# Four batches through a gated block and a spectral block: first blocks of all batches, then second blocks, with split weights kept in DRAM

## The chip, the core and the metric

One core of a Trainium2 chip runs the whole kernel. The metric is the device time of one execution in microseconds (us); lower is better. Kernels are compared by the median of several executions.

## What is computed

Batch B = 4, sequence S = 768, model width 384 (8 heads of 48), in three steps, all in float32:

```python
# attention: a decayed state per head
f = 1 / (1 + exp(-f_logit))
for t in range(S):
    state = f[:, :, t, :, None] * state + einsum('bhd,bhde', k[:, :, t], v[:, :, t])
    y[:, :, t] = einsum('bhd,bhde->bhe', q[:, :, t], state)
# first block
h = gelu_tanh(x @ w_in)                         # 384 -> 1024
u, v = h[..., :512], h[..., 512:]
v_n = layernorm(v) * g_ln
v_s = einsum('ts,bsd->btd', w_sg, v_n) + b_sg   # mixes tokens, 768 x 768
x = x + (u * v_s) @ w_out                       # 512 -> 384
# second block
theta = x @ w_theta
y = einsum('ts,bsd->btd', w_tok_r, x * cos(theta)) + einsum('ts,bsd->btd', w_tok_i, x * sin(theta))
u = x + y
out = u + maximum(u @ w_ch, 0)
```

w_in, w_out, w_theta, w_tok_r, w_tok_i and w_ch reach the chip as 64-bit floats, w_sg as 32-bit ones.

## The kernel before, in words

**Split products.** A float32 product is made of three matmuls of fp32r parts: every operand is split into a rounded part (hi, an ACT cast) and what is left over (lo, a DVE subtraction), and `mm3` (lines 771 to 785) adds hi x hi, hi x lo and lo x hi in PSUM (lines 779, 780, 781). A split weight is twice as large as the weight itself.

**Weights.** `load_f32` (411) brings a weight tile in; 64-bit ones land in a raw buffer and are turned into float32 by an ACT operation (431) and four DVE ones (432 to 435). `load_split` (437) adds the cast (444) and the subtraction (445). `w_in` and `w_out` are split once and stay in SBUF (`win`, `wout`). The mixing weights don't fit: they pass as 36 tiles of 128 x 384 for each batch (`order`, 394: 12 tiles `g` of w_sg, 24 of w_tok_r and w_tok_i), through `stream` (481) into the five slots of `st`. The 24 are decoded once by `decode` (474), from a raw slot into a float32 slot `wt` (two slots), and written to `scratch1` in DRAM by POOL's queue; each batch then loads them (192 KB, `dt<-scratch`) and splits them anew, as it does with the tiles of w_sg (`dt<-in_w_sgT`). So 144 tiles are split in all. `channel_weights` (460) makes w_theta and w_ch for the first batch that needs them, keeps both parts in `scratch2`, and loads them from there for the others into the one slot `wmid`.

**A first block** (`block1`, 926) runs p1 (v half of x @ w_in with gelu and layernorm, six token tiles), p2(0), p3(0) (token mixing, 12 matmuls on each streamed tile), p2(1), p4(0) (w_out and the residual), p3(1), and hands back p4(1) as a call, which the next block runs in its middle (`before`). The layernorm's power is a POOL operation (975). **A second block** (`block2`, 1003) runs theta (sine and cosine, an ACT chain of lines 881 to 888 and DVE products of line 891), p6(0) and p6(1) (token mixing, 216 matmuls in all, 9 on each streamed tile), and p7 with the output DMA. x lives in `xst` (two slots for each half of the sequence), its split parts in `X`. **Attention** of a batch is two halves of four head pairs (`unit`, 585, one mask multiply of line 657 in each); its results go to `xst` by DMAs of POOL (752).

**Order.** Nothing is ordered by hand. The operations of all engines are created with a due time `vt` (the due times of a block's products add up in `mm3`), and `schedule` (173) plays them on a model of the engines: each engine takes, of the operations that can start at its next free moment, the one with the earliest due time, so work without hurry fills idle time. A DMA of POOL is counted as 1.05 us of issue, and lands 0.65 + bytes / 360e3 + 0.95 us later (lines 283 to 290, 400). The engines then run their lists strictly in this order, each instruction behind the one before it. The buffers of one kind are taken in the order in which they were created.

Lines 1042 to 1076 say what is created, in which order: attention of batch 0; first block of 0, with attention of 1 spread beside it; first block of 1; decoding, spread from the start of batch 0's block over 80% of both blocks; second block of 0; second block of 1, with attention of 2 beside it; then batch 2, both blocks, with attention of 3 beside them; then batch 3. The two calls that decide:

```python
        rest = one1(rest, False)
...
            decode(pl, g, i, v + (pl.vt - v) * at / 100)
        two(rest, True)
...
        two1(nothing, True)
        x = spread(2, v)
```

A second program branch (`general`, 1089) for very small decays is built too and is not run with these inputs.

Of the kernel before, what the change touches and what calls it, by code (L numbers as in the profile page):

```python
# [8 lines left out]
F32 = mybir.dt.float32  # L9
# [39 lines left out]
WARM_GAP = 0.3  # L49
N_DT = 3  # L50
N_W = 2
# [3 lines left out]
MID = 90.0  # L55
# [268 lines left out]
def body(tc, ctx, att, qkv, flog, w_in, g_ln, w_sgT, b_sg, w_out, w_theta, w_rT, w_iT, w_ch, out):  # L324
# [86 lines left out]
    def load_f32(pl, g, dst, src, vt, after=(), background=False):  # L411

        n = src.shape[-1]
        d, get = dst
        if src.dtype != I64:
            dma(pl, "SP", n * 512, lambda: nc.sync.dma_start(get(), src), after, w=[d], vt=vt - 3)
            return
# [19 lines left out]
    def load_split(pl, g, hi, lo, his, src, vt, scale=None, after=(), background=False):  # L437

        n = src.shape[-1]
        t = pl.buf(g.w32 if background else g.dt, [P, TH])  # L440
        load_f32(pl, g, (t, lambda: t.t[:, :n]), src, vt, after, background)
        if scale is not None:
            pl.op("ACT", a1(n), lambda: nc.scalar.mul(t.t[:, :n], t.t[:, :n], scale), [], [t], vt=vt)
        pl.op("ACT", a1(n), lambda: nc.scalar.copy(his()[0], t.t[:, :n]), [t], [], hi, vt=vt)  # L444
        pl.op("DVE", v1(n), lambda: nc.vector.tensor_sub(his()[1], t.t[:, :n], his()[0].bitcast(F32)), [t, *hi], [], lo, vt=vt)  # L445

    def weights_in(pl, g, cs, vt):
        for c in cs:
            for k in range(NK):
                cc, b = slice(c * WC, (c + 1) * WC), [g.win[k][c]]  # L450
                load_split(
                    pl, g, b, b, lambda k=k, cc=cc: (win[:, 0, k, cc], win[:, 1, k, cc]), w_in[k * P : (k + 1) * P, cc], vt,
                )

    def weights_out(pl, g, vt):
        for k in range(ND):
            b = [g.wout[k]]
            load_split(pl, g, b, b, lambda k=k: (wout[:, 0, k], wout[:, 1, k]), w_out[k * P : (k + 1) * P], vt)

    def channel_weights(pl, g, i, b, vt):  # L460
        w = pl.buf(g.wmid, [P, 2, NK, DM], F32R)
        if b == 0:
            src, scale = ((w_theta, 1.0 / (2.0 * math.pi)), (w_ch, None))[i]
            for k in range(NK):
                load_split(
                    pl, g, [w], [w], lambda k=k: (w.t[:, 0, k], w.t[:, 1, k]), src[k * P : (k + 1) * P], vt, scale,
                    background=True,
                )
            dma(pl, "POOL", P * 9216, lambda: nc.gpsimd.dma_start(scratch2[i], w.t.bitcast(F32)), [w], [g.scr2[i]], vt=vt)
        else:  # L470
            dma(pl, "SP", P * 9216, lambda: nc.sync.dma_start(w.t.bitcast(F32), scratch2[i]), [g.scr2[i]], [w], vt=vt)
# [294 lines left out]
    def moe(pl, g, xst, get, wmid, out_b, pace, first=False):  # L766
# [34 lines left out]
        def residual(ps, hf, k, resplit=True):  # L801
# [48 lines left out]
        def p4(hf, gb, resplit):  # L850
            for c in range(NK):
# [5 lines left out]
                residual(ps, hf, c, resplit)  # L857
# [68 lines left out]
        def block1(before, resplit):  # L926
# [72 lines left out]
            p4(0, g0, resplit)  # L999
            g1 = p3(1, u1, vtiles)  # L1000
            return lambda: p4(1, g1, resplit)
# [26 lines left out]
    with tc.manual_schedule():  # L1028
# [15 lines left out]

        def blocks(b, x):
            get = lambda pl, i: stream(pl, g, i, pl.vt - LEAD)
            wmid = lambda pl, i: mids.pop() if mids else channel_weights(pl, g, i, b, pl.vt - LEAD * 1.5)
            return moe(pl, g, x, get, wmid, out[b], PACE if b + 1 < B else 1.0, b == 0)
# [5 lines left out]
        v = pl.vt  # L1054
        one, two = blocks(0, x)
        rest = one(nothing, False)
        x = spread(1, v + (pl.vt - v) * LATE / 100)
        one1, two1 = blocks(1, x)
        rest = one1(rest, False)
        mids = []  # L1060
        for i in range(2 * NS, len(order)):
            at = BG_FROM + (BG_TO - BG_FROM) * (i - 2 * NS) / (len(order) - 2 * NS)
            if not mids and at >= MID:
# [156 lines left out]
```

## Time and profile before

| | |
|---|---|
| median of 3 runs | 686.87 us (684.5 to 708.57) |
| the profiled execution's own time | 685.9 us |
| its span, first to last instruction | 684.2 us |
| mean granted TensorE clock | 0.974 of full |
| TensorE matmul busy | 626.0 us (91%) |
| VectorE busy | 512.5 us (75%) |
| ScalarE busy | 398.1 us (58%) |
| GpSimd busy | 82.4 us (12%) |

| stretch of the span (us) | what TensorE runs in it |
|---|---|
| 0 to 77.1 | attention of batch 0, decoding of w_in, first p1 tiles of batch 0, and p2(0) |
| 77.1 to 174.8 | the rest of batch 0's first block but p4(1), attention of batch 1 |
| 174.8 to 243.2 | first block of batch 1, p4(1) of batch 0 |
| 243.2 to 314.1 | second block of batch 0, p4(1) of batch 1, some attention of batch 2 |
| 314.1 to 403.0 | second block of batch 1, the rest of batch 2's attention |
| 403.0 to 471.2 | first block of batch 2, half of batch 3's attention |
| 471.2 to 550.0 | second block of batch 2, p4(1), the other half |
| 550.0 to 607.0 | first block of batch 3 |
| 607.0 to 684.2 | second block of batch 3 with p4(1) and theta (to 630.3), p6 (to 668.0), p7, last stores |

The engines are PE (TensorE matmuls), PEld (its weight loads), DVE (VectorE), ACT (ScalarE), POOL (GpSimd) and SP (which only issues DMAs). PEclk is the TensorE clock that was granted, 1.00 being the full 2.4 GHz. An instruction's line is that of the helper that records it. Matmuls are pipelined: of 128x384 ones each shows some 0.34 us, and one ends every 0.17 us.

### The profile page before, as it was taken

The numbers are of one execution on the slowest core, as the hardware profiler recorded it, in microseconds if no ns is written. First come the engines' busy times: TensorE is split into PE (matmuls) and PEld (weight loads), VectorE is DVE, ScalarE is ACT, GpSimd is POOL, SyncE is SP. The second block draws the span as 40 slices with busy tenths as digits, with TensorE's granted clock in tenths as the row PEclk, the third lists the DMA queues.
The fourth block names the chain that finished last, engine by engine and source line by source line (L and its number), as shares of the span: only waits on it lengthen the run. The fifth ranks groups of instructions, "written<-read, shape, count | busy, mean of one in ns | idle before, by whom it ended". The sixth has DMA issues, their size and how long they took to land.

```text
span 684.2 us, 15430 instructions
## 1 busy us (share of the span) xinstructions
PE 626.0 (91%) x5997; PEld 579.0 (85%) x5997; DVE 512.5 (75%) x1185; ACT 398.1 (58%) x839; POOL 82.4 (12%) x148
## 2 busy tenths in 40 slices
PE   8778878879898999997999999999999999989996
PEld 8667657768698989996898888999899989988995
DVE  6999999899899899666866596867865553667533
ACT  6757596744874567563854658645754365347520
POOL 2001213225021000102001212011000100000000
PEclk9999989898999999998999999999999999999999
DMA  8534638279365520647154563222243341021422
GB/s 327 189 105 120 244 117 313 71 215 309 102 185 174 181 86 38 190 144 242 36 185 120 186 197 107 88 77 86 79 148 102 109 141 46 24 69 49 138 70 74
DMA packets 43506, 93.77 MB, mean 137 GB/s; under 512 B 6112, under 2 KB 29600, under 8 KB 42400
## 3 DMA queue, kind: packets, MB, share of 16 engines
q1 hardware_dynamic: 35360, 64.18, 30.3%
q0 software_dynamic: 8064, 28.52, 12.2%
q8 instruction: 49, 0.80, 0.5%
q14 instruction: 33, 0.27, 0.2%
HBM read 76.15 MB, written 11.80 MB: 129 GB/s over the span
## 4 chain that ended last, share of the span: by engine, by line
PE 52%; DVE 23%; ACT 8%; DMA 8%; issue 7%; POOL 1%; SPq 0%; ACTq 0%; DVEq 0%; POOLq 0%
PE mm L779 17%; PE mm L781 16%; PE mm L780 16%; DMA dt<-in_w_sgT 2%; DMA f<-in_flog 2%; ACT L312 2%; DVE ar L789 1%; DMA xst<-y 1%; DVE s L677 1%; DMA wmid<-scratch 1%; DVE s L682 1%; DVE am L657 1%; ACT tmp L887 1%; DVE tmp L891 1%; DVE wt L434 1%
## 5 line engine op out<-in xcount | busy, mean ns | idle before, releaser
L779 PE MATMUL mm<-st,ar 128*128 128x384 f32 x480 | 167.9, 350 | 0.0
L780 PE MATMUL mm<-st,ar 128*128 128x384 f32 x480 | 162.2, 338 | 0.7 <-DVE st L445 0.7
L781 PE MATMUL mm<-st,ar 128*128 128x384 f32 x480 | 162.1, 338 | 0.0
L444 ACT CAST st<-dt 128x384 fp32r<-128x384 f32 x144 | 72.7, 511 | 98.7 <-PE mm L781 53.6
L445 DVE TENSOR_TENSOR st<-dt,st 128x384 fp32r<-128x384 f32 x144 | 76.9, 553 | 70.0 <-ACT st L444 69.7
L779 PEld LDWEIGHTS mm<-st,ar 128*128 128x128 f32 x480 | 91.2, 190 | 3.4 <-DVE tmp L884 0.3
L780 PEld LDWEIGHTS mm<-st,ar 128*128 128x128 f32 x480 | 91.4, 191 | 1.2 <-DVE st L445 1.1
L781 PEld LDWEIGHTS mm<-st,ar 128*128 128x128 f32 x480 | 91.2, 190 | 0.0
L798 ACT CAST x<-xst 128x384 fp32r<-128x384 f32 x72 | 35.9, 511 | 41.2 <-DVE xst L803 21.3
L799 DVE TENSOR_TENSOR x<-xst,x 128x384 fp32r<-128x384 f32 x72 | 38.4, 553 | 7.0 <-ACT x L798 6.5
L788 ACT CAST ar<-tmp 128x384 fp32r<-128x384 f32 x80 | 38.7, 509 | 7.7 <-DVE tmp L844 6.7
L789 DVE TENSOR_TENSOR ar<-tmp,ar 128x384 fp32r<-128x384 f32 x80 | 41.1, 551 | 0.9 <-ACT ar L788 0.4
L752 POOL DMA_DIRECT2D xst<-y x60 | 30.3, 509 | 77.0 <-ACT y L729 57.2
L803 DVE TENSOR_TENSOR xst<-xst,mm 128x384 f32<-128x384 f32 x48 | 25.6, 550 | 17.8 <-PE mm L781 17.6
L779 PE MATMUL mm<-x,win 128*128 128x384 f32 x96 | 35.3, 368 | 2.8 <-DVE tmp L839 2.6
L779 PE MATMUL mm<-ar,wout 128*128 128x384 f32 x96 | 33.3, 347 | 4.0 <-DVE tmp L891 3.4
L779 PE MATMUL mm<-win,x 128*128 128x512 f32 x72 | 29.4, 409 | 6.1 <-ACT x L798 3.5
L687 ACT ACTIVATE s<-s,bends 128x48 f32<-128x48 f32 x64 | 20.7, 333 | 23.4 <-DVE s L677 22.4
L781 PE MATMUL mm<-x,win 128*128 128x384 f32 x96 | 33.9, 354 | 0.4 <-DVE win L445 0.4
L780 PE MATMUL mm<-x,win 128*128 128x384 f32 x96 | 33.8, 352 | 0.0
L781 PE MATMUL mm<-ar,wout 128*128 128x384 f32 x96 | 32.3, 336 | 1.2 <-DVE wout L445 1.2
L780 PE MATMUL mm<-ar,wout 128*128 128x384 f32 x96 | 32.3, 336 | 0.1
(156 smaller groups left out, 1401.6 us busy)
## 6 DMA issues: line engine op xcount, KB each, us to landing
dt<-scratch SPq DMA_DIRECT2D x96, 192.0 KB, 2.5
qkv<-in_qkv POOLq DMA_DIRECT2D x24, 536.0 KB, 5.6
dt<-in_w_sgT SPq DMA_DIRECT2D x48, 192.0 KB, 3.7
wmid<-scratch SPq DMA_DIRECT2D x6, 1152.0 KB, 5.6
raw<-in_w_rT SPq DMA_DIRECT2D x12, 384.0 KB, 3.8
raw<-in_w_iT SPq DMA_DIRECT2D x12, 384.0 KB, 4.5
scratch<-wt POOLq DMA_DIRECT2D x24, 192.0 KB, 4.2
f<-in_flog POOLq DMA_DIRECT2D x6, 768.0 KB, 5.6
```

The source lines that it names most:

```text
L444: pl.op("ACT", a1(n), lambda: nc.scalar.copy(his()[0], t.t[:, :n]), [t], [], hi, vt=vt)
L445: pl.op("DVE", v1(n), lambda: nc.vector.tensor_sub(his()[1], t.t[:, :n], his()[0].bitcast(F32)), [t, *hi], [], lo, vt=vt)
L687: "ACT", 0.23, lambda: nc.scalar.activation(s2(), s1(), AF.Copy, scale=be[:, c // 2 : c // 2 + 1]), r=[bb, fulls[c // 2]], w=[b2]
L752: lambda r0=r0, n=n, kc=kc, o=64 * j + off: q[yq].dma_start(xst.t[r0 : r0 + n, kc], y.t[o : o + n].rearrange("p i a t -> p (i a t)")),
L779: nc.tensor.matmul(o, h0, h1, start=start, stop=False)
L780: nc.tensor.matmul(o, h0, l1, start=False, stop=False)
L781: nc.tensor.matmul(o, l0, h1, start=False, stop=stop)
L788: pl.op("ACT", a1(n), lambda: nc.scalar.copy(tiles()[0], src.t[:, :n]), [src], [hi])
L789: pl.op("DVE", v1(n), lambda: V.tensor_sub(tiles()[1], src.t[:, :n], tiles()[0].bitcast(F32)), [src, hi], [lo])
L798: pl.op("ACT", a1(TH), lambda: nc.scalar.copy(X[hf][:, 0, k], T()), [src], [hi])
L799: pl.op("DVE", v1(TH), lambda: V.tensor_sub(X[hf][:, 1, k], T(), X[hf][:, 0, k].bitcast(F32)), [src, hi], [lo])
L803: pl.op("DVE", v1(TH), lambda: V.tensor_add(T(), T(), ps.t[:, :TH]), [ps], [xst[hf].parts[k]])
```

## The change

All four first blocks come one behind the other, with the attention of the next batch beside each but the last. Then come the second blocks, batch 3's first, then those of 0, 1 and 2. The x of batches 0, 1 and 2 is stored in DRAM (`xs`) when its first block's residual is done, by DMAs of POOL, and loaded again for its second block by SP.

`scratch1` now holds both parts of each tile. Batch 0's `g` tiles are split when they are first used, and written; `decode` splits its tile and writes both parts; every other use of a tile is one 384 KB load straight into `st`. Decoding and `channel_weights` are spread from the end of batch 0's first block over 80% of the time up to the end of batch 3's. Both pass through the `dt` slots, and `wt`, now twice as large, has one slot. For the second blocks both channel weights are loaded once, into `win`, which the first blocks no longer need then.

```diff
-N_W = 2
+N_W = 1
-MID = 90.0
...
-    scratch1 = dr.tile([36, P, TH], F32, name="scratch1")
+    scratch1 = dr.tile([36, P, 2, TH], F32, name="scratch1")
+    xs = dr.tile([B, 2, NK, P, TH], F32, name="xs")
...
-    def load_split(pl, g, hi, lo, his, src, vt, scale=None, after=(), background=False):
+    def load_split(pl, g, w, his, src, vt, scale=None, background=False):
...
-        t = pl.buf(g.w32 if background else g.dt, [P, TH])
+        d = pl.buf(g.dt, [P, TH])
...
+    def channel_load(pl, g, i, vt, place=None):
+        w = pl.buf(g.wmid, [P, 2, NK, DM], F32R) if place is None else Buf(t=win[:, :, :, place * DM : (place + 1) * DM])
+        old = [] if place is None else [x for xs_ in g.win for x in xs_]
+        dma(pl, "SP", P * 9216, lambda: nc.sync.dma_start(w.t.bitcast(F32), scratch2[i]), [g.scr2[i]], [w, *old], vt=vt)
         return w
 
     def decode(pl, g, i, vt):
         m, s, t = order[i]
-        w = pl.buf(g.w32, [P, TH])
+        w = pl.buf(g.w32, [P, 2, TH], F32R)
         src = srcs[m][s * P : (s + 1) * P, t * TH : (t + 1) * TH]
-        load_f32(pl, g, (w, lambda: w.t), src, vt, background=True)
-        dma(pl, "POOL", P * 1536, lambda: nc.gpsimd.dma_start(scratch1[i], w.t), [w], [g.scr1[i]], vt=vt)
-
-    def stream(pl, g, i, vt):
-        m, s, t = order[i]
-        src = srcs[m][s * P : (s + 1) * P, t * TH : (t + 1) * TH]
+        load_split(pl, g, w, lambda: (w.t[:, 0], w.t[:, 1]), src, vt, background=True)
+        dma(pl, "POOL", P * 3072, lambda: nc.gpsimd.dma_start(scratch1[i], w.t.bitcast(F32)), [w], [g.scr1[i]], vt=vt)
+
+    def stream(pl, g, i, vt, new=False):
         w = pl.buf(g.st, [P, 2, TH], F32R)
-        his = lambda: (w.t[:, 0], w.t[:, 1])
-        if m == "g":
-            load_split(pl, g, [w], [w], his, src, vt)
+        if new:
+            m, s, t = order[i]
+            src = srcs[m][s * P : (s + 1) * P, t * TH : (t + 1) * TH]
+            load_split(pl, g, w, lambda: (w.t[:, 0], w.t[:, 1]), src, vt)
+            dma(pl, "POOL", P * 3072, lambda: nc.gpsimd.dma_start(scratch1[i], w.t.bitcast(F32)), [w], [g.scr1[i]], vt=vt + 4.0)
         else:
-            load_split(pl, g, [w], [w], his, scratch1[i], vt, after=[g.scr1[i]])
+            dma(pl, "SP", P * 3072, lambda: nc.sync.dma_start(w.t.bitcast(F32), scratch1[i]), [g.scr1[i]], [w], vt=vt)
         return w
...
+            if keep is not None:
+                b, done = keep
+                dma(pl, "POOL", P * TH * 4, lambda: nc.gpsimd.dma_start(xs[b, hf, k], T()), [xst[hf].parts[k]], [done[hf][k]])
...
+        rest, last, kept = nothing, B - 1, {}
+        for b in range(B):
+            v = pl.vt
+            one, two = blocks(b, x)
+            kept[b] = [[Buf() for _ in range(NK)] for _ in range(2)]
+            rest = one(rest, b == last, (b, kept[b]) if b != last else None)
+            if b == 0:
+                va = pl.vt
+            if b != last:
+                x = spread(b + 1, v + (pl.vt - v) * (LATE / 100 if b == 0 else 0.0))
+        n = len(order) - 2 * NS
+        for i in range(n):
+            if i in (n // 3, 2 * n // 3):
+                channel_weights(pl, g, i // (n // 3) - 1, va + (pl.vt - va) * (BG_FROM + (BG_TO - BG_FROM) * i / n) / 100)
+            decode(pl, g, 2 * NS + i, va + (pl.vt - va) * (BG_FROM + (BG_TO - BG_FROM) * i / n) / 100)
+        mids = [channel_load(pl, g, i, pl.vt - 8.0, i) for i in range(2)]
+        for b in (last, *range(last)):
+            if b != last:
+                x = []
+                for hf in range(2):
+                    t = pl.buf(g.xst[hf], [P, NK, TH])
+                    t.parts = [Buf(of=t) for _ in range(NK)]
+                    x.append(t)
+                    for k in range(NK):
+                        dma(
+                            pl, "SP", P * TH * 4, lambda t=t, b=b, hf=hf, k=k: nc.sync.dma_start(t.t[:, k], xs[b, hf, k]),
+                            [kept[b][hf][k]], [t.parts[k]], vt=pl.vt - 20.0,
+                        )
+                two = blocks(b, x)[1]
+            two(rest, b != last)
+            rest = nothing
         pl.emit()
```

## Rows read from the trace of the kernel before

**Rows 1.** The page: the span, busy times, DVE by 40 slices, GB/s by slices.
```profile
span 684.2 us, 15430 instructions
...
PE 626.0 (91%) x5997; PEld 579.0 (85%) x5997; DVE 512.5 (75%) x1185; ACT 398.1 (58%) x839; POOL 82.4 (12%) x148
...
DVE  6999999899899899666866596867865553667533
...
GB/s 327 189 105 120 244 117 313 71 215 309 102 185 174 181 86 38 190 144 242 36 185 120 186 197 107 88 77 86 79 148 102 109 141 46 24 69 49 138 70 74
```

**Rows 2.** Windows: stretch, its length, busy of each engine, PEclk, DMA share, GB/s.
```profile
77.10:174.80 97.70, 77.79 (x1006) 66.93 (x1004) 89.90 (x206) 59.33 (x113) 27.28 (x48) 0.88 0.69 223
174.80:243.20 68.40, 65.20 (x343) 61.33 (x343) 63.32 (x142) 43.80 (x92) 7.73 (x12) 0.98 0.51 157
...
403.00:471.20 68.20, 67.95 (x673) 62.37 (x672) 48.80 (x110) 40.31 (x85) 9.49 (x15) 1.00 0.35 107
...
550.00:607.00 57.00, 57.00 (x313) 54.84 (x312) 26.59 (x56) 26.11 (x59) 1.73 (x2) 1.00 0.22 66
...
630.30:668.00 37.70, 37.70 (x219) 37.66 (x218) 19.30 (x38) 16.25 (x35) 0.00 (x0) 1.00 0.37 116
...
200.00:250.00 50.00, 48.09 (x312) 47.14 (x311) 47.15 (x101) 26.70 (x55) 4.39 (x7) 0.97 0.51 160
...
607.00:677.40 70.40, 67.34 (x383) 64.55 (x382) 42.99 (x87) 34.06 (x70) 0.00 (x0) 1.00 0.25 80
403.00:550.00 147.00, 145.85 (x1445) 134.80 (x1444) 102.72 (x231) 84.22 (x181) 16.05 (x28) 1.00 0.35 106
550.00:677.40 127.40, 124.34 (x695) 119.39 (x693) 69.58 (x142) 60.18 (x129) 1.73 (x2) 1.00 0.24 74
```

**Rows 3.** Chain that ended last: start, length, what.
```profile
135.45 1.87 DVE ar L789 x4
...
314.37 7.69 DMA wmid<-scratch
```

**Rows 4.** Windows of line 657, the attention's mask multiply.
```profile
403.00:471.20 68.20, 2.20 (x4) 1.00 0.35 107
471.20:550.00 78.80, 2.20 (x4) 1.00 0.35 105
```

**Rows 5.** Groups by line and shape: busy, mean ns of one, idle before.
```profile
L445 DVE TENSOR_TENSOR st<-dt,st 128x384 fp32r<-128x384 f32 x144 | 76.9, 553 | 70.0 <-ACT st L444 69.7
L444 ACT CAST st<-dt 128x384 fp32r<-128x384 f32 x144 | 72.7, 511 | 98.7 <-PE mm L781 53.6 <-DMA dt<-scratch 31.7 <-DMA dt<-in_w_sgT 9.9
...
L574 DVE TENSOR_TENSOR_SCAN f<-f,seed 128x1536 f32<-128x1536 f32 x6 | 20.1, 3358 | 0.2
```

**Rows 6.** Windows of tile wt: busy of DVE, ACT and POOL on it.
```profile
48.70:77.10 28.40, 5.17 (x12) 1.13 (x2) 1.75 (x3) 1.00 0.42 124
77.10:174.80 97.70, 23.27 (x48) 6.62 (x12) 6.89 (x13) 0.88 0.69 223
...
sum 684.20, DVE 58.75 ACT 20.99 POOL 13.80; mean DVE 4.90 ACT 1.75 POOL 1.15
```

**Rows 7.** Windows of line 445, the subtraction of the split.
```profile
550.00:607.00 57.00, 5.48 (x10) 1.00 0.22 66
```

**Rows 8.** DMA issues: count, KB each, median us from issue to landing.
```profile
dt<-scratch SPq DMA_DIRECT2D x96, 192.0 KB, 2.5
...
raw<-in_w_iT SPq DMA_DIRECT2D x12, 384.0 KB, 4.5
scratch<-wt POOLq DMA_DIRECT2D x24, 192.0 KB, 4.2
...
out<-xst SPq DMA_DIRECT2D x24, 192.0 KB, 2.4
...
scratch<-wmid POOLq DMA_DIRECT2D x2, 1152.0 KB, 5.6
```

**Rows 9.** Waits: who waited for whom, us in total, times, longest.
```profile
ACT wt L431 <- DMA scratch<-wt: 5.3, 5, 2.0
```

More of the change, by code (lines that the diff above doesn't have):

```diff
@@ L369, in make_state @@
         g.w32, g.raw = Slots(main, "wt", N_W), Slots(main, "raw", N_RAW)
+        g.dt = Slots(main, "dt", N_DT)
         g.tmp = Slots(main, "tmp", N_TMP)
-        g.dt = Slots(main, "dt", N_DT)
         g.u = Slots(main, "u", N_U)
@@ L449, in weights_in @@
             for k in range(NK):
-                cc, b = slice(c * WC, (c + 1) * WC), [g.win[k][c]]
+                cc = slice(c * WC, (c + 1) * WC)
                 load_split(
-                    pl, g, b, b, lambda k=k, cc=cc: (win[:, 0, k, cc], win[:, 1, k, cc]), w_in[k * P : (k + 1) * P, cc], vt,
+                    pl, g, g.win[k][c], lambda k=k, cc=cc: (win[:, 0, k, cc], win[:, 1, k, cc]), w_in[k * P : (k + 1) * P, cc], vt,
                 )
@@ L848, in p3, with p4 @@
             return gb
-        def p4(hf, gb, resplit):
+        def p4(hf, gb, resplit, keep):
             for c in range(NK):
@@ L856, in p4 @@
                     mm3(ps, ((w, w), lambda d=d, cc=cc: (wout[:, 0, d, cc], wout[:, 1, d, cc])), gb[d], d == 0, d == ND - 1, TH)
-                residual(ps, hf, c, resplit)
+                residual(ps, hf, c, resplit, keep)
         Z = {}
@@ L924, in p7, with block1 @@
                 )
-        def block1(before, resplit):
+        def block1(before, resplit, keep=None):
             xsplits((0,) if first else (0, 1))
@@ L998, in block1 @@
             u1 = p2(1)
-            p4(0, g0, resplit)
+            p4(0, g0, resplit, keep)
             g1 = p3(1, u1, vtiles)
-            return lambda: p4(1, g1, resplit)
+            return lambda: p4(1, g1, resplit, keep)
         def block2(before, resplit):
@@ L1043, in body @@
         pl.vt = DENSE
+        mids = []
         def blocks(b, x):
-            get = lambda pl, i: stream(pl, g, i, pl.vt - LEAD)
-            wmid = lambda pl, i: mids.pop() if mids else channel_weights(pl, g, i, b, pl.vt - LEAD * 1.5)
-            return moe(pl, g, x, get, wmid, out[b], PACE if b + 1 < B else 1.0, b == 0)
+            get = lambda pl, i: stream(pl, g, i, pl.vt - LEAD, b == 0 and i < 2 * NS)
+            return moe(pl, g, x, get, lambda pl, i: mids[i], out[b], PACE, b == 0)
@@ L1050, in spread @@
         def spread(b, v):
             return attention(pl, g, b, v + (pl.vt - v) * ATT_FROM / 100, v + (pl.vt - v) * ATT_TO / 100)
[L1054 to L1063, printed above, removed]
-                mids = [channel_weights(pl, g, 0, 0, v + (pl.vt - v) * MID / 100)]
-            decode(pl, g, i, v + (pl.vt - v) * at / 100)
@@ L1066, in body @@
-        two(rest, True)
-        v = pl.vt
-        two1(nothing, True)
-        x = spread(2, v)
-        for b in (2, 3):
+        rest, last, kept = nothing, B - 1, {}
+        for b in range(B):
             v = pl.vt
             one, two = blocks(b, x)
-            two(one(nothing, True), False)
-            if b == 2:
-                x = spread(3, v)
+            kept[b] = [[Buf() for _ in range(NK)] for _ in range(2)]
[4 more added lines that the diff above has]
+                x = spread(b + 1, v + (pl.vt - v) * (LATE / 100 if b == 0 else 0.0))
@@ new lines, in body @@
+        n = len(order) - 2 * NS
[11 more added lines that the diff above has]
+                    x.append(t)
+                    for k in range(NK):
+                        dma(
+                            pl, "SP", P * TH * 4, lambda t=t, b=b, hf=hf, k=k: nc.sync.dma_start(t.t[:, k], xs[b, hf, k]),
+                            [kept[b][hf][k]], [t.parts[k]], vt=pl.vt - 20.0,
+                        )
+                two = blocks(b, x)[1]
+            two(rest, b != last)
+            rest = nothing
@@ L1140, in general @@
             g = make_state(False)
+            weights_in(pl, g, range(DFF // WC), 0.0)
             xin = []
```

38 lines of the change are left out of this document (16 added, 22 removed).

## The prediction

> **What bounds the kernel now.** I read the page's totals first: 684.2 us of span, and TensorE matmuls busy for 91% of it [rows 1]. The row of DVE slices says more: VectorE stands at 9 tenths from the third slice to the fourteenth, and then falls to 5 to 8 [rows 1]. So I cut the span by stages with the windows view [rows 2]. Batch 3's two blocks (550 to 677.4) have neither attention nor decoding beside them: 57.0 for the first block, 70.4 for the second, in which its own leftover p4(1) is run; TensorE is busy 124.3 of 127.4. Batch 2 with all of batch 3's attention (403 to 550) takes 147.0 with TensorE busy 145.9. These stages go at TensorE's pace, with the granted clock at full. The stretch from 77.1 to 174.8 (rest of batch 0's first block, batch 1's attention, decoding) does not: DVE is busy 89.9 of 97.7, PE 77.8 at a granted clock of 0.88 of full. From 174.8 to 243.2 (batch 1's first block, decoding, no attention) DVE has 63.3 of 68.4; 50 us in it (200 to 250) have 47.2. So before 250 us VectorE sets the pace, behind that TensorE does. One stall stands apart: 7.7 us for the channel weights at 314 [rows 3].
>
> TensorE's needs, for the sums below: 36 split products of p4(1) take 216 products' time over 6, 37.7 / 6 = 6.3 (630 to 668 holds p6's 216). A first block behind another one also runs the other's p4(1): 57.0 + 6.3 = 63.3. Attention beside a first block: 403 to 471.2 holds half of it (four of eight mask multiplies [rows 4]) and takes 68.2 against 57.0, so 2 x 11.2 = 22.4 per batch.
>
> **Part by part.** *Splits dropped.* 144 cast-and-subtract pairs on streamed weights become 36 (12 in batch 0's first block, 24 while decoding): 108 x 0.53 = 57 us of DVE and 108 x 0.50 = 55 of ACT go [rows 5]. In the second blocks this buys nothing: in p6, PE was busy for 37.70 of 37.70 us with them in place [rows 2]. I take 0 there; the bound on a gain is the 3.1 us that PE idled in 550 to 677.4, per batch.
>
> *Decoding moved.* It leaves batch 0's first block: the `wt` operations there are 23.3 of DVE's 89.9 [rows 6]. They return between batch 0's first block and 80% of the way to the end of batch 3's, 24 of them with a subtract more. All of it: 58.8 [rows 6] + 24 x 0.53 = 71.5 of DVE. Spread over 0.8 x 3 = 2.4 blocks, 2 / 2.4 of it, 59.6, lies in the first blocks of batches 1 and 2.
>
> *Attention moved.* Batch 2's used to lie beside second blocks, batch 3's over both of batch 2's blocks; now each lies wholly beside one first block. Its DVE time is 102.7 - 69.6 = 33.1 [rows 2], and one scan of 3.4 that fell before 403 [rows 5]: 36.5. A bare first block's DVE time is 26.6 [rows 2] less ten splits, 5.5 [rows 7], less three re-splits of x (1.6, which only the last batch still does), plus what falls outside the window: twelve operations of the second half's gating (5.6, at the 0.47 at which such operations follow each other, four in 1.87 [rows 3]), three residual adds and three entry splits (3): 28.
>
> *Stage A, to the end of batch 2's first block.* DVE from 77.1 on: batch 0 89.9 - 23.3 = 66.6; batches 1 and 2 2 x (28 + 36.5) + 59.6 = 188.6; sum 255. TensorE over the same: about 66 for batch 0 (57.0 less half of p1 and a p2, 13, plus 22.4) and 2 x (63.3 + 22.4) = 171, sum 237. DVE is the larger. Before, it was busy 0.926 (174.8 to 243.2) to 0.943 (200 to 250) of the time where it set the pace; I take 0.935: 255 / 0.935 = 273. The start moves from 77.1 to about 73 (four of the 5.2 us of `wt` operations from 48.7 to 77.1). Stage A ends at 346.
>
> *Stage B.* Batch 3's first block, its DVE need 28 + 12 + 2, is TensorE's again: 63.3, to 409. Its second: 70.4. The other three have no p4(1): 64.1, and 1 for entry splits that wait for the last p7: 65.1 each, 195.3. Then the tail of 6.8 as now (677.4 to 684.2): 409 + 70.4 + 195.3 + 6.8 = 681.5. This leaves out the stall at 314, since both channel weights now stay in `win`, with no reload: batch 3's rows have none either.
>
> *x kept and loaded.* 18 stores of 192 KB on POOL and as many loads on SP. An SP store of that size lands in 2.4, a POOL one in 4.2 [rows 8]; each load is given a due time 20 us ahead, its buffer being free a block before. I take 0. If the cover fails, a batch's first load is late by up to 4, three times: 0 to +12. On POOL the stores stand ahead of the rsqrt (L975) and of the attention's copies, so a store that waits for a residual holds these back; with POOL at 12% of the span [rows 1] I take 0, at most +6.
>
> *Bytes.* A streamed tile is now 384 KB, not 192. In p6 24 of them pass in 37.7 us: 9.44 MB, 250 GB/s. The busiest slice moved 327 [rows 1], and a 384 KB load landed in 4.5 under load [rows 8]; five `st` buffers hold 5 x 1.57 = 7.9 us of work. I take 0; the upper end is the third rival's.
>
> *One `wt` slot.* A decode's cast now waits until the previous write has landed. Behind the waiting cast stand all of ACT's later operations, and DVE's subtract. I take 0 beyond the 0.935; the price is the second rival's.
>
> Sum: 681.5 of span + 1.7 (the profiled execution's 685.9 less its 684.2) = **683 us**, against 685.9, or 686.9 for the median shown. The 37 us by which VectorE holds up the first blocks of batches 0 and 1 now (97.7 - 66 and 68.4 - 63.3) are not removed: 36 (273 - 237) come back, spread over three batches.
>
> **Rivals.** *1: TensorE sets stage A.* If attention, decoding and first block interleave so well that DVE's need is no bound (its slices of 9 hold decodes pulled forward into idle time), stage A is 237, and the 5.1 that batch 1's block lost (68.4 - 63.3) comes twice: 683 - 273 + 247 = 657. For it: 200 to 250 had PE busy 48.1 and DVE 47.2 at once. Against it: from 77.1 to 174.8, with attention, PE needed about 66 and took 97.7.
>
> *2, slower: the one slot stops ACT.* The planner counts a 384 KB write on POOL as 1.05 + 0.65 + 1.09 + 0.95 = 3.7 us (lines 283 to 290 and 400). Measured: 4.2 for 192 KB, 5.6 for 1152 KB [rows 8], so 0.5 to 1.9 more than planned; at 1.2, 24 casts hold ACT and then DVE for 29 us in the stage where DVE has none to spare: 712. It decides as soon as casts are planned tight behind the slot. For it: with two slots ACT already waited 5.3 us in 5 of its waits [rows 9]. Against it: a cycle of cast, subtract and landing is about 6.7, and stage A leaves over 8 per decode.
>
> The Trainium skill (SBUF — State Buffer, "SBUF: two separate sides") says that a DMA issued from POOL cannot have its descriptors written while a VectorE operation holds the shared port pair. The rows fit that: a store of 192 KB took 4.2 from POOL and 2.4 from SP [rows 8]. By that rule writes in the DVE-full stage would land later than the rows' medians, by up to one VectorE operation (0.55), 24 x 0.55 = 13: 696. It is a part of rival 2, weaker than its price, and has its share of that chance.
>
> *3: p6 waits for its tiles.* If transfers reach only the 223 GB/s of 77.1 to 174.8 (share 0.69 [rows 2]), 9.44 MB take 42.3, 4.6 more than now, four times: 701. For it: the need of 250 is above any 50 us mean in the rows. Against it: slices of 309 to 327.
>
> **Numbers.** Forecast 0.46, rival 1 0.29, rival 2 0.16, rival 3 0.09. About 2% either way (673 and 701) can be told from no change. The forecast's own range is 671 to 695 (DVE share 0.975 to 0.895): a sixth of it is below 673. Faster: 0.07 + 0.26 = 0.33; slower: nearly all of rival 2, half of rival 3, a little of the forecast: 0.21; same 0.46. The range takes in rival 1's time and the lower half of rival 2's: 655 to 708.
>
> **What would show it.** Right: DVE at 9 tenths until about 345 us, batches 1 and 2 at about 100 us a first block; four second blocks of 64 to 71 with PE full in p6; `st` splits 12, not 144; no gap for channel weights. Rival 1: first blocks of 86 to 90. Rival 2: a large sum of ACT waits on the DMA `scratch<-wt`. Rival 3: PE waits on the DMA of `st`. Wrong altogether: a second block well under 64, or PE stalls between blocks.

## The result, and the profile after

The changed kernel takes 676.1 us (median of 4 runs, 675.9 to 677.7), against 686.7 for the kernel before in runs beside it: a ratio of 0.986 (95% interval 0.983 to 0.989). Its profiled execution took 677.7 us with a span of 676.0. One of the four runs of the kernel before, at 708.6, was in a slow state that the others were not in, and the ratio leaves it out.

The page of the changed kernel: span, busy times, slices of PE, DVE and ACT, and what the DMA engines moved.

```profile
span 676.0 us, 15027 instructions
...
PE 616.3 (91%) x5953; PEld 569.8 (84%) x5953; DVE 453.6 (67%) x1077; ACT 342.3 (51%) x728; POOL 99.5 (15%) x178
...
PE   8788688989999988988989999899999999999996
...
DVE  6999778969999897889979333741482175148203
ACT  6658587646685665675536421740291055019200
...
GB/s 331 190 84 74 285 120 217 120 264 270 170 252 248 245 258 270 147 245 250 173 264 212 144 190 182 23 165 253 207 77 277 252 154 156 252 219 25 250 194 76
```

VectorE lost 59 us of work (512.5 in [rows 1]) and ScalarE 56, and the span lost 8. DVE's 9s now end at the twenty-second slice (372 us); behind it the slices read 0 to 8. The windows view of the same kernel shows where the time went; the stretches are: rest of batch 0's first block, first blocks of 1, 2 and 3, batch 3's second block up to p6, p6 and p7, second blocks of 0, 1 and 2.

```profile
75.40:162.40 87.00, 69.72 (x990) 59.74 (x988) 71.58 (x165) 58.21 (x107) 26.07 (x47) 0.90 0.61 204
162.40:255.40 93.00, 85.42 (x1100) 75.88 (x1101) 85.91 (x204) 61.86 (x127) 29.82 (x51) 1.00 0.75 244
255.40:353.70 98.30, 88.02 (x1094) 77.08 (x1093) 85.18 (x209) 55.69 (x122) 25.45 (x44) 0.97 0.66 221
353.70:420.00 66.30, 66.07 (x350) 62.45 (x351) 33.37 (x75) 24.79 (x59) 6.22 (x10) 0.97 0.56 188
420.00:442.20 22.20, 19.27 (x112) 17.78 (x110) 17.36 (x37) 15.95 (x33) 0.00 (x0) 1.00 0.09 31
442.20:490.90 48.70, 48.70 (x283) 48.64 (x282) 16.57 (x33) 11.39 (x25) 0.00 (x0) 1.00 0.70 220
490.90:550.90 60.00, 59.13 (x344) 57.91 (x343) 26.80 (x55) 22.56 (x48) 0.00 (x0) 1.00 0.65 201
550.90:610.90 60.00, 59.14 (x344) 57.97 (x343) 26.79 (x55) 22.54 (x49) 0.00 (x0) 1.00 0.61 190
610.90:669.40 58.50, 57.65 (x334) 56.14 (x332) 24.43 (x50) 19.59 (x43) 0.00 (x0) 1.00 0.46 146
```

Stage by stage, with the stretches of the table and of [rows 2]:

| | before | after | difference |
|---|---|---|---|
| to the end of batch 0's first block (without p4(1)) | 174.8 | 162.4 | -12.4 |
| first block of batch 1 (before: no attention beside it) | 68.4 | 93.0 | +24.6 |
| first block of batch 2 (before: half of batch 3's attention) | 68.2 | 98.3 | +30.1 |
| first block of batch 3 (now with p4(1) of batch 2) | 57.0 | 66.3 | +9.3 |
| the four second blocks | 309.0 | 249.4 | -59.6 |
| tail | 6.8 | 6.6 | -0.2 |

The four second blocks were 70.9, 88.9, 78.8 and 70.4 and are now 70.9, 60.0, 60.0 and 58.5. Read from the bottom: the second blocks give 59.6 back, and the later first blocks take 64.0, for the attention and the p4(1) that used to lie in second blocks. From the end of batch 0's first block on, the changed kernel is 4.2 us slower than the one before (513.6 against 509.4). Its 12.4 us are won ahead of that point, where the decoding is gone; behind it, it has the decoding to do.

The DMA issues of the changed kernel (KB each, median us to landing), beside [rows 8]:

```profile
st<-scratch SPq DMA_DIRECT2D x132, 384.0 KB, 3.8
...
scratch<-wt POOLq DMA_DIRECT2D x24, 384.0 KB, 4.1
...
scratch<-st POOLq DMA_DIRECT2D x12, 384.0 KB, 6.7
out<-xst SPq DMA_DIRECT2D x24, 192.0 KB, 2.0
xs<-xst POOLq DMA_DIRECT2D x18, 192.0 KB, 3.0
xst<-xs SPq DMA_DIRECT2D x18, 192.0 KB, 3.3
```

And its waits (us in total, times, longest): the two that rivals 2 and 3 spoke of, and TensorE's longest in products (a PSUM buffer that VectorE's gating, line 845, had still to read):

```profile
ACT wt L445 <- DMA scratch<-wt: 8.6, 8, 2.3
...
PE mm L782 <- DVE tmp L845: 6.1, 3, 3.0
...
PE mm L782 <- DMA st<-scratch: 2.4, 1, 2.4
```

PE waited once, for 2.4 us, for a tile of `st`. In p6 and p7 of batch 3 (442.2 to 490.9) it was busy without a gap, at 220 GB/s over the stretch.

### The profile page after: what moved, and what is told of

Read it like the earlier page. It is cut to its first block, busy times and chain, and to the rows that moved or that the text cites. A ratio compares the mean times of both kernels' runs of the same rounds, so it can differ in the third digit from the quotient of the medians.

```text
span 676.0 us, 15027 instructions
## 1 busy us (share of the span) xinstructions
PE 616.3 (91%) x5953; PEld 569.8 (84%) x5953; DVE 453.6 (67%) x1077; ACT 342.3 (51%) x728; POOL 99.5 (15%) x178
## 4 chain that ended last, share of the span: by engine, by line
PE 42%; DVE 23%; ACT 11%; DMA 11%; issue 9%; POOL 2%; SPq 0%; DVEq 0%; POOLq 0%; ACTq 0%
PE mm L782 14%; PE mm L783 13%; PE mm L784 13%; DMA f<-in_flog 3%; DMA scratch<-wt 3%; DMA dt<-in_w_sgT 2%; DMA raw<-in_w_iT 2%; DVE s L680 2%; DVE dt L434 1%; DVE dt L435 1%; ACT ar L791 1%; DVE s L685 1%; DVE am L660 1%; POOL xst L755 1%; DVE tmp L845 1%
## 5 line engine op out<-in xcount | busy, mean ns | idle before, releaser
L782 PE MATMUL mm<-win,x 128*128 128x512 f32 (+1 forms) x144 | 56.6, 393 | 7.4 <-DVE tmp L845 3.7
L782 PE MATMUL mm<-x,win 128*128 128x384 f32 x168 | 58.4, 348 | 0.0
L784 PE MATMUL mm<-win,x 128*128 128x512 f32 (+1 forms) x144 | 54.1, 376 | 3.0 <-DVE x L802 3.0
L784 PE MATMUL mm<-x,win 128*128 128x384 f32 x168 | 56.3, 335 | 0.0
L783 PE MATMUL mm<-x,win 128*128 128x384 f32 x168 | 56.2, 335 | 0.0
L783 PE MATMUL mm<-win,x 128*128 128x512 f32 (+1 forms) x144 | 53.5, 372 | 0.1
L782 PE MATMUL mm<-ar,wout 128*128 128x384 f32 x96 | 35.6, 371 | 4.2 <-DVE tmp L845 2.4
L782 PEld LDWEIGHTS mm<-win,x 128*128 128x128 f32 x144 | 27.8, 193 | 13.1 <-DVE tmp L845 5.4
L784 PE MATMUL mm<-ar,wout 128*128 128x384 f32 x96 | 33.3, 347 | 1.1 <-DVE wout L446 1.1
L783 PE MATMUL mm<-ar,wout 128*128 128x384 f32 x96 | 33.4, 348 | 0.4 <-DVE ar L792 0.4
```

The source lines that it names most:

```text
L782: nc.tensor.matmul(o, h0, h1, start=start, stop=False)
L783: nc.tensor.matmul(o, h0, l1, start=False, stop=False)
L784: nc.tensor.matmul(o, l0, h1, start=False, stop=stop)
```

## The experiments

Two theories stood at first. Theory 1: VectorE's load sets the first blocks with attention, TensorE the second blocks, and the dropped splits bring nothing there. Theory 2: the second blocks are shorter because ScalarE and VectorE no longer split in them. As the runs came in, a third question took over: what sets the first blocks of batches 1 and 2, since VectorE's load does not.

Two things limit what the stretches below can show. Each comes from one profiled execution, and executions of one kernel differ by up to 10 us (680.1 to 689.6 in experiment 9). And neighbouring blocks overlap: a few p1 products of the next run ahead of the last p3 products of the one before, so a border between two blocks can be put several us earlier or later. The end of all four first blocks is clearer; a table behind experiment 12 has it for each kernel.

**1. The order alone.**

```diff
-N_W = 1
+N_W = 2
...
-    scratch1 = dr.tile([36, P, 2, TH], F32, name="scratch1")
+    scratch1 = dr.tile([36, P, TH], F32, name="scratch1")
...
-            dma(pl, "SP", P * 3072, lambda: nc.sync.dma_start(w.t.bitcast(F32), scratch1[i]), [g.scr1[i]], [w], vt=vt)
+            load_split(pl, g, [w], [w], his, scratch1[i], vt, after=[g.scr1[i]])
...
```

Every use of a tile splits it again, `decode` writes whole tiles, and `wt` has two slots, as before the change.

> The new order of blocks alone: scratch1 holds whole tiles again and each use splits them (144 splits, none while decoding). Theory 1 (VectorE sets the first blocks, TensorE the second ones, where splits are hidden): the second blocks keep the 60.0 us of the changed kernel; the first blocks of batches 1, 2 and 3 take 12 splits each more on VectorE (6.4 us) and lose 10 decode subtractions (5.3 us), so stage A ends within 5 us of the changed kernel's 354 and the whole is 674 to 682. Theory 2 (the second blocks are shorter because ScalarE and VectorE no longer split there): each of the three second blocks returns to about 65 us and the whole is 690 or more.

Measured: 678.7 us, ratio 0.994 (0.990 to 0.997). Its windows, for the rest of batch 0's first block, the first blocks of batches 1 and 2 and two of the second blocks:

```profile
75.00:163.00 88.00, 72.34 (x988) 61.70 (x986) 77.25 (x178) 60.34 (x111) 24.16 (x41) 0.86 0.58 191
163.00:255.20 92.20, 84.47 (x1090) 74.54 (x1090) 83.61 (x194) 59.80 (x124) 27.76 (x47) 1.00 0.54 176
255.20:355.00 99.80, 88.98 (x1105) 78.68 (x1103) 85.89 (x213) 58.08 (x128) 26.35 (x45) 0.97 0.54 173
...
492.00:552.00 60.00, 59.15 (x344) 57.94 (x343) 39.47 (x79) 34.05 (x73) 0.00 (x0) 1.00 0.39 121
552.00:612.10 60.10, 59.26 (x346) 58.03 (x344) 39.75 (x80) 33.89 (x74) 0.00 (x0) 1.00 0.38 114
```

The second blocks take 60.0 and 60.1 with 13 us more of VectorE work in each. Theory 2 falls. The splits were hidden behind TensorE, as they were in p6 before. The ratio lies above that of the changed kernel and the intervals don't meet, each beside its own runs of the kernel before; but the two profiled executions differ by 1.0 us only, in no stage by more than 1.5. Whether the 0.7% come from the dropped splits, or from the new plan that any edit brings (experiment 9), is not settled.

**2. The splits alone, in the old order.**

```diff
-N_DT = 3
-N_W = 2
+N_DT = 2
+N_W = 1
...
-    scratch1 = dr.tile([36, P, TH], F32, name="scratch1")
+    scratch1 = dr.tile([36, P, 2, TH], F32, name="scratch1")
...
-        g.w32, g.raw = Slots(main, "wt", N_W), Slots(main, "raw", N_RAW)
+        g.wd, g.w32, g.raw = Slots(main, "wd", 1), Slots(main, "wt", N_W), Slots(main, "raw", N_RAW)
...
```

> Both parts kept in DRAM alone, in the old order of blocks (one dt slot less, a slot of its own for the whole tile). Theory 1: the decode subtractions, 24 x 0.53 = 13 us, come into the stretch before 250 us that VectorE sets, the 12 splits of batch 1's first block (6 us) leave it; nothing is gained where TensorE sets the pace: 686 to 696. Theory 2: 96 splits fewer beside second blocks and 24 beside later first blocks shorten these, 5 us a batch: 665 to 675.

Measured: 705.2 us, ratio 1.032 (1.026 to 1.038): slower than either theory had it. Windows of the rest of batch 0's first block and of batch 0's second block, and one of PE's waits:

```profile
76.50:190.30 113.80, 87.42 (x1020) 73.06 (x1018) 97.50 (x227) 70.49 (x133) 35.97 (x63) 0.84 0.73 254
...
258.00:344.50 86.50, 75.41 (x548) 71.20 (x548) 48.42 (x108) 35.49 (x75) 2.65 (x5) 0.91 0.59 194
```
```profile
PE mm L779 <- ACT wmid L444: 7.3, 3, 3.4
```

Batch 0's block grew from 97.7 to 113.8 [rows 2] and the granted clock in it fell to 0.84. Later the channel weights came late, and TensorE waited 7.3 us for them. From its first p1 product to that of the next, batch 2 was 1.8 us shorter than before (145.4 against 147.2), and batch 3 took 126.4 to the end of its last product, against 127.5. So in the old order the dropped splits, with the single slots that they need here, cost more than they bring. How much of the 16 us is VectorE's extra work, and how much those slots, was not separated.

**3. Decoding later.** `BG_TO` from 80 to 100.

> The changed kernel with decoding spread over 100% instead of 80% of the way to the end of batch 3's first block. If VectorE's load sets the first blocks of batches 1 and 2, a sixth of the decoding (0.17 x 71 = 12 us) moves to batch 3's first block, where VectorE has 33 of 66 us idle: stage A ends 8 to 13 us sooner, batch 3's block is unchanged, the whole 663 to 669. If something else sets them (the attention's chain of latencies, ScalarE stops on the one slot), 672 to 678.

Measured: 676.9 us, ratio 0.992 (0.989 to 0.994). It tells little: the two blocks' VectorE work hardly changed (84.2 and 85.3, against 85.9 and 85.2), because the planner puts decodes wherever an engine is free, whatever their due time.

```profile
163.50:257.00 93.50, 84.64 (x1091) 74.45 (x1091) 84.24 (x199) 60.91 (x124) 28.65 (x49) 1.00 0.71 237
257.00:351.40 94.40, 86.39 (x1103) 76.35 (x1103) 85.27 (x207) 55.55 (x121) 26.72 (x45) 1.00 0.70 228
```

**4. Less VectorE work.** So the work itself was taken away (lines 432, 433 and 435 left out of background decodes).

```diff
-    op(v2(n), lambda: V.tensor_scalar(get(), get(), TINY, None, ALU.max))
-    op(v2(n), lambda: V.tensor_scalar(iget(), iget(), 3, 0x3FFFFFFF, ALU.logical_shift_left, ALU.bitwise_and))
+    if not background:
+        op(v2(n), lambda: V.tensor_scalar(get(), get(), TINY, None, ALU.max))
+        op(v2(n), lambda: V.tensor_scalar(iget(), iget(), 3, 0x3FFFFFFF, ALU.logical_shift_left, ALU.bitwise_and))
...
```

> The changed kernel without three of the four VectorE operations in each decode of a mixing or channel weight (the lower bound, the shift with mask and the low bits are left out, so the weights are wrong): 30 x 1.24 = 37 us less of VectorE, 31 of them before 354 us; waits on slots and DMAs stay. If VectorE's load sets stage A, it falls by 20 to 33 us (TensorE needs about 240 of its 278): 644 to 657. If the attention's latencies or the slot set it, by less than 8: 668 to 676.

Measured: 670.2 us, ratio 0.981 (0.975 to 0.986). Its first blocks of batches 1 and 2:

```profile
163.70:253.30 89.60, 84.39 (x1091) 74.40 (x1092) 76.48 (x175) 61.08 (x128) 29.71 (x51) 1.00 0.81 275
253.30:345.60 92.30, 86.49 (x1108) 76.89 (x1108) 69.47 (x170) 57.26 (x127) 26.02 (x46) 1.00 0.75 244
```

VectorE's work there fell by 25 us (171.1 to 146.0) and the two blocks by 9.4 (191.3 to 181.9). VectorE is now busy 0.80 of them. Its load alone does not set them. (The profiled execution took 667.7 us, the only other one 672.7.)

**5. Less TensorE work**, by leaving the third product out of p3.

```diff
-                nc.tensor.matmul(o, l0, h1, start=False, stop=stop)
+                if not two:
+                    nc.tensor.matmul(o, l0, h1, start=False, stop=stop)
...
```

> The changed kernel with the third product (lo x hi) left out of every token mixing of the first blocks, 48 of 144 matmuls a batch: 8.4 us less of TensorE in each first block, nothing less on the other engines (the result loses accuracy). Batch 3's first block is TensorE's, so it falls by 8.4 in any case. If TensorE's own need (85 of the 93 to 98 us it is busy) sets batches 1 and 2, each falls by 6 to 8 as well and the whole is 650 to 656. If VectorE's or the attention's chain sets them, each falls by 0 to 3 and the whole is 660 to 668.

Measured: 667.8 us, ratio 0.974 (0.970 to 0.979). Rest of batch 0's first block, then the first blocks of batches 1, 2 and 3:

```profile
75.10:165.00 89.90, 66.17 (x939) 56.24 (x938) 73.95 (x165) 58.40 (x107) 25.93 (x45) 0.80 0.56 190
165.00:254.50 89.50, 80.79 (x1054) 69.47 (x1053) 79.25 (x192) 60.41 (x123) 28.41 (x48) 0.98 0.71 242
254.50:353.20 98.70, 81.39 (x1056) 69.77 (x1056) 89.15 (x222) 57.29 (x126) 26.74 (x47) 0.97 0.68 235
353.20:408.20 55.00, 54.47 (x297) 51.86 (x296) 34.07 (x75) 24.40 (x59) 6.91 (x11) 1.00 0.66 228
```

With these borders batch 3's block, the control, fell by 11.3 and the other two together by 3.1 of 16.8. The borders decide here: the first p1 product of batch 3 starts at 353.2 (353.7 in the changed kernel), but the last p3 product of batch 2 ends at 353.4 (361.3). Over all four first blocks, 33.6 us of matmuls were left out and the end came 13.5 sooner (408.2 for 421.7). So TensorE's load does not set the whole stage alone, but it is worth more than 3.1. A part was lost to the clock: in batch 0's stretch the granted clock fell from 0.90 to 0.80, and of the 33.6 TensorE's busy time fell by 25.6 in all (616.3 to 590.7).

**6. Both cuts at once**, to see whether each load hid behind the other.

> Both cuts at once: three VectorE operations left out of each decode (31 us of VectorE before the end of stage A) and the third product left out of the first blocks' token mixing (8.4 us of TensorE a block); the result is wrong. Alone they shortened the first blocks of batches 1 and 2 together by 9 and by 3 us. If TensorE and VectorE are two nearly equal bounds there, each hidden behind the other, the two blocks fall together by 22 to 30 us, and the whole, with 8 to 11 from batch 3's block, is 637 to 646. If a chain of latencies through the attention sets them, the cuts only add up, 12 us or less, and the whole is 653 to 661.

Measured: 656.1 us, ratio 0.959 (0.948 to 0.970). First blocks of batches 1 and 2, and the shares of the chain of waits between 165 and 344 us:

```profile
165.60:260.00 94.40, 83.79 (x1074) 71.85 (x1078) 73.03 (x171) 62.74 (x130) 28.87 (x51) 0.95 0.78 266
260.00:344.40 84.40, 78.63 (x1039) 69.27 (x1032) 67.25 (x166) 54.75 (x122) 24.86 (x44) 0.97 0.74 242
```
```profile
by line: DMA raw<-in_w_rT 9.4%; DMA f<-in_flog 9.0%; DMA st<-scratch 8.1%; issue 6.9%; PE mm L784 4.4%; PE mm L785 3.8%; DMA raw<-in_w_iT 3.5%; DMA scratch<-wt 3.1%; ACT f L571 2.5%; ACT f L570 2.4%; DVE dt L435 2.2%; DVE ar L796 2.2%; DVE 
```

Together they fell by 12.5 (191.3 to 178.8), as the 9.4 and 3.1 add up to; that it fits so closely is luck, since the profiled execution was the slower of two (659.0 and 653.1) and experiment 4's the faster. By the end of all four first blocks the two cuts together are worth 20.3 us, alone 11.1 and 13.5: by either reading less than, or no more than, the sum. Two bounds hidden behind each other would have given 22 to 30 in the two blocks. By the medians of whole runs, each against the kernel before, the two cuts stand at 1.9% and 2.6% alone and 4.1% together, the changed kernel at 1.4%; the last interval is too wide to tell a sum from somewhat more. The granted clock, 0.95 and 0.97 here against 1.00 and 0.97, took some of it back. Five kinds of DMA landings make 33% of the chain (9.4 + 9.0 + 8.1 + 3.5 + 3.1); the rest is work of the engines one behind another, and issue.

**7. Two `wt` slots** (`N_W = 2`; the channel weights pass through `wt` as well, which frees `wmid`).

> The changed kernel with two wt slots instead of one; the room comes from the wmid slot, as the channel weights are now decoded piece by piece through wt too. If ScalarE's waits for the landing of scratch<-wt (8.6 us in the changed kernel) hold up the first blocks, these go and the whole is 666 to 672. If they lie beside other work: 673 to 679.

Measured: 677.1 us (runs from 670.8 to 681.1), ratio 0.985 (0.979 to 0.991): nothing that can be told from the changed kernel. The waits did not go altogether:

```profile
ACT wt L445 <- DMA scratch<-wt: 5.0, 2, 3.2
```

So this run by itself does not show that they lie beside other work; experiment 11 bears on it.

**8. Two buffers for the decay tile** (`N_F = 2`, same room).

> The changed kernel with two buffers for the attention's decay tile f (room from wmid, as in the run with two slots, but one wt slot): the load and the sigmoid of a half no longer wait for the last pair of the half before. If the start of each half (load 4.8, four ACT passes of 1.5, scan 3.4) holds up the first blocks of batches 1 and 2 or the end of batch 0's: 662 to 670. If VectorE or TensorE is full meanwhile anyway: 673 to 679.

Measured: 670.3 us, ratio 0.976 (0.971 to 0.982). Rest of batch 0's first block, then the first blocks of 1, 2 and 3:

```profile
75.50:158.30 82.80, 66.56 (x983) 56.44 (x981) 70.31 (x163) 56.77 (x104) 25.21 (x43) 0.94 0.62 213
158.30:252.00 93.70, 87.04 (x1096) 76.83 (x1096) 87.87 (x205) 67.22 (x130) 31.42 (x54) 0.98 0.74 251
252.00:353.00 101.00, 92.51 (x1121) 82.37 (x1121) 88.76 (x220) 55.81 (x127) 28.17 (x48) 0.97 0.70 225
353.00:414.50 61.50, 61.50 (x341) 59.37 (x340) 31.00 (x68) 22.97 (x56) 6.53 (x10) 1.00 0.54 180
```

A gain, at the upper edge of the first theory. Where it lies depends on the border again. By these stretches batch 0's is 4.2 shorter, batch 3's block 4.8, and batches 1 and 2 are 3.4 longer. By the last p3 product of each block batches 1 and 2 are 11.6 shorter (188.0 for 199.6) and the others longer. The end of all four comes 6.9 sooner.

**9. Attention due earlier.** `ATT_TO` from 100 to 88.

> The changed kernel with each batch's attention due at 88% of the first block beside it, not 100%. If TensorE waits at the hand-over to the next first block for the attention's last pairs (it is idle for 3 us at 351 and at half clock for some after), this goes in two or three places: 668 to 673. If the earlier due time only moves the same work: 674 to 680.

Measured: 684.2 us, ratio 1.000 (0.996 to 1.004). No engine has more or less to do, and the whole gain is gone; batch 2's first block takes 103.4. How the planner interleaves the same work is worth as much as the change itself, and every edit here brings a new plan, so a gain of a few us in one experiment is not yet the gain of its idea.

**10. Decoding from the start again.**

```diff
-N_DT = 3
+N_DT = 2
...
-        d = pl.buf(g.dt, [P, TH])
+        d = pl.buf(g.wd if background else g.dt, [P, TH])
...
             if b == 0:
-                va = pl.vt
+                va = v
```

> The changed kernel with decoding spread from the start of batch 0's first block again, as before the change (whole tiles get a slot of their own, one dt slot less). If the decoding beside batch 0's attention and weights is what cost 10 us from 77 to 175 in the kernel before, batch 0's block grows by 10 to 20 us, and of this batches 1 and 2 give back 4 to 10 as they decode a fifth less: 679 to 692. If its place doesn't matter: 672 to 679.

Measured: 684.3 us, ratio 1.001 (0.997 to 1.005). Rest of batch 0's first block, then the first blocks of 1 and 2:

```profile
76.50:172.70 96.20, 76.07 (x1010) 63.85 (x1011) 86.18 (x198) 64.20 (x120) 33.31 (x59) 0.93 0.72 244
172.70:267.00 94.30, 89.00 (x1158) 78.17 (x1157) 86.54 (x203) 63.25 (x128) 29.54 (x50) 1.00 0.74 250
267.00:357.80 90.80, 84.16 (x1040) 73.91 (x1036) 77.74 (x191) 52.97 (x116) 25.94 (x44) 0.98 0.62 205
```

Batch 0's first block ends at 172.7 in place of 162.4, and batches 1 and 2 give 6.2 back. With the decoding beside batch 0's block, nothing of the gain can be measured. This kernel also has one slot less for `dt`, so a part of it may be that; and its profiled execution was the fastest of ten (679.9), its span only 2.2 us above the changed kernel's. Experiment 1 has the slots of the kernel before and decodes late: there the stretch took 88.0, against 97.7 [rows 2]. In the eleven kernels here that decode late, batch 1's first product starts at 156.7 to 166.1 us; in the three that decode from the start, at 172.7 to 190.6.

**11. Two `f` buffers and two `wt` slots.**

> The changed kernel with two buffers for f and two wt slots, both in the room of wmid. Two f buffers gave 670, two wt slots alone nothing that can be told from 676. If the slot doesn't matter: 667 to 673, as with two f buffers alone. If the two together free ScalarE (which waited 20.9 us for scratch<-wt with two f buffers): 660 to 667.

Measured: 667.1 us, ratio 0.977 (0.969 to 0.986). It beats the kernel before and, by its interval, can't be told from experiment 8; by their medians these two are the fastest kernels here that do the whole computation. ScalarE waited 1.2 us for `scratch<-wt`, against the 20.9 of experiment 8, and no gain clear of the noise came of it. That, more than experiment 7, shows that the slot's waits lie beside other work.

**12. Later landings in the planner's model.**

```diff
-                o.end = dev + 0.95
+                o.end = dev + 2.2
```

> The changed kernel, but the planner counts 2.2 us in place of 0.95 for the end of each DMA. Measured beside attention and decoding: 4.5 us for a 384 KB st tile that it counts with 3.2, 4.8 for the 72 KB pieces of attention that it counts with 2.9, 5.4 for raw tiles it counts with 3.2. No work changes, only the order of instructions. If instructions placed tight behind a landing, which then stop their engine and all behind it, set the first blocks of batches 1 and 2 (both engine loads cut gave only 12 us there, and the chain of the run with both cut holds a third of DMA landings), these fall by 8 to 15 us: 661 to 668. If not: 673 to 680.

Measured: 672.1 us, ratio 0.979 (0.974 to 0.985). Rest of batch 0's first block, first blocks of 1 and 2:

```profile
75.50:165.50 90.00, 72.61 (x990) 62.86 (x988) 71.49 (x164) 58.46 (x107) 26.71 (x46) 0.87 0.60 202
165.50:256.50 91.00, 87.45 (x1150) 76.97 (x1150) 84.88 (x205) 63.18 (x128) 28.89 (x49) 1.00 0.76 254
256.50:352.10 95.60, 87.35 (x1062) 76.88 (x1062) 85.93 (x215) 56.22 (x122) 26.06 (x45) 1.00 0.66 220
```

By these stretches the two blocks are 4.7 shorter (186.6); by the first p1 products, 9.9 (181.4), which the first theory would claim. The whole lies between the theories, and its interval meets the changed kernel's (0.983 to 0.989). With what a new plan does by itself (experiment 9), it is not shown that landings later than planned hold these blocks up.

**All together.** The end of the last p3 product of batch 3 is where all four first blocks are done, but for p4(1). Experiments 2 (the old order) and 7 (profiled in the slowest of its runs, 681.1) have no row:

| kernel | end (us) | against the changed kernel |
|---|---|---|
| the changed kernel | 421.7 | |
| 1, splits at each use | 422.8 | +1.1 |
| 3, decoding due later | 420.0 | -1.7 |
| 4, 33 us less VectorE work | 410.6 | -11.1 |
| 5, 33.6 us less TensorE work | 408.2 | -13.5 |
| 6, both | 401.4 | -20.3 |
| 8, two `f` buffers | 414.8 | -6.9 |
| 9, attention due earlier | 424.8 | +3.1 |
| 10, decoding from the start | 423.8 | +2.1 |
| 11, two `f` buffers and two `wt` slots | 409.6 | -12.1 |
| 12, later landings in the plan | 415.1 | -6.6 |

Experiments 3 and 9 change no work, so 2 to 3 us either way at this point, and 1.4% of the whole in experiment 9's median, are what a new plan can do. Taking away a load brings a third to two fifths of it.

## Why the prediction was right, and where its steps were not

The forecast was 683 us, just below the kernel before, with a range of 655 to 708; it came out at 676. The direction held, and the reason for a small gain in part. That it came so near is luck: stage A ended 7.7 later than forecast, batch 3's two blocks took 3.5 more, and the other three second blocks 16.8 less.

*Splits dropped: 0 in the second blocks.* Held, shown by experiment 1: 60.0 with them, 60.0 without.

*Decoding moved.* The step that earns the gain, as far as the runs show: batch 0's stretch is 9.7 to 10.7 shorter with late decoding and the slots as they were or one fewer (experiment 1, changed kernel). That the whole gain goes without it (experiment 10) is weaker, since experiment 9 loses it too with the decoding late. Its size was off: by the forecast's own terms batch 0's part of stage A ends at 73 + 66.6 / 0.935 = 144, 31 us sooner than before; measured it ends at 162.4, 12.4 sooner. VectorE had 71.6 to do there, not 66.6, and was busy 0.82 of the time, not 0.935; TensorE's clock stood at 0.90.

*Stage A: VectorE sets the pace.* This step failed. Its end was forecast at 346 and measured at 353.7, near enough, but by wrong factors: VectorE's work was 242.7 (71.6 + 85.9 + 85.2), not 255, and it was busy 0.87 of the stage, not 0.935. Batch 0's 18 us too many and the other two blocks' 11 too few made up for each other. Experiment 4 shows that VectorE's load alone does not set the first blocks of batches 1 and 2, and experiments 5 and 6 that TensorE's alone does not set the stage. TensorE's need, by my own sum 171 of the 191.3 us, is the nearest floor under them. I read 0.93 busy as the mark of a bound; with attention, 0.92 and 0.87 stood beside a load that could be cut by 25 us for 9.4. (The row of DVE slices, too, I read too short: 8s and 9s stand from the second to the sixteenth slice [rows 1], to 274 us.)

*Batch 3's first block: 63.3.* Measured 66.3, of which 2.9 stands at the hand-over (TensorE ends a product of batch 2's p3 at 350.8 and starts batch 3's p1 at 353.7, behind the gating's wait of 3.0; batch 2's last nine p3 products follow at 359.5).

*The other second blocks: 65.1.* Mis-sized: 60.0, 60.0 and 58.5, 17 us in all. I took away p4(1)'s 6.3 (36 matmuls, which I called 36 split products) and added 1 for the entry splits. But of the 3.1 us that TensorE idled in [rows 2], 2.2 went with p4(1). The longest of them stood right before its first product:

```profile
616.19 0.44 PE L779 MATMUL mm<-ar,wout 128*128 128x384 f32 x1 [1.50 <-DVE tmp L891]
```

TensorE idles 0.9 in a block of 60.0 now. I had named these 3.1 as the bound on a gain and then priced them at 0. The 1 for entry splits did not come, and TensorE's busy time fell by 8.2 (67.3 to 59.1), 1.9 more than p4(1)'s matmuls; no run takes these 1.9 apart.

*x kept, loads, bytes, one slot: 0.* Held. No wait for `xst<-xs` is among PE's, a 384 KB tile landed in 3.8, and the waits for the one slot, 8.6 and not 29, gave nothing clear of the noise when they were cut (experiments 7 and 11), so rival 2 falls. Rival 3 falls with PE's single wait of 2.4 for a tile of `st`. Rival 1's sign, first blocks of 86 to 90, did not come (93.0 and 98.3): TensorE's pace was not reached in stage A.

The Trainium skill (SBUF — State Buffer, "SBUF: two separate sides") would have POOL's writes land late while VectorE holds the shared ports. The rows leave it open: in the changed kernel twice the bytes landed in 4.1 us from POOL, with VectorE busy nine tenths of the time in stage A's later blocks; before, 192 KB took 4.2. But the twelve writes of batch 0's split tiles, as large and from POOL too, took 6.7, most of them where VectorE was busy 0.82. No run separates VectorE's part from that of the other transfers.

*Open.* What sets the first blocks of batches 1 and 2, 20 us above TensorE's need. TensorE was idle for 17.9 of the 191.3 us. Of these 6.1 and 2.4 are the waits shown with the result, and most of the rest was spent in attention:

```profile
PE at L703 <- DVE s L680: 4.6, 5, 1.6
...
PE at L639 <- ACT kt L631: 2.2, 2, 1.5
PE at L703 <- DVE s L685: 2.1, 4, 1.0
```

So 12.8 us of it were waits for VectorE: for the attention's state (lines 680 and 685) and for the gating (line 845). Since taking VectorE work away brought only a third of it, when VectorE got to these operations may count more than how much it had to do; this is argued, not shown. The attention's chain from pair to pair was not tried by itself.

## What to carry to other kernels

An engine at nine tenths is not yet a bound: take work away from it, and see whether the stage follows, at a border that the blocks beside it don't blur. Price a stage that loses a part by taking away that part's stalls too, not only its work. Where a planner orders in-order queues, change something that moves no work first, as in experiment 9, to learn how much a new plan alone is worth; a smaller gain than that shows nothing yet.

## What had not been expected

A due time moved by 12% (experiment 9) costs 1.4%, with the same work on every engine. TensorE's granted clock fell where its work was cut: with a third of p3's matmuls gone (experiment 5) it was 0.80 in batch 0's stretch, where it had been 0.90, and the stretch took 89.9 in place of 87.0. And in the first 17 us behind 75.4, TensorE had 7.5 us of work, while the granted clock was 0.69 and DMAs moved 288 GB/s, the batch's attention inputs among them: the next place to look in this kernel.

```profile
75.40:92.00 16.60, 7.47 (x25) 5.54 (x24) 10.22 (x16) 12.13 (x16) 1.10 (x3) 0.69 0.78 288
```
